# mLSTM attention and softplus feed-forward in one kernel: new places for the parts of the feature-major steps

## The chip, the cores and the metric

The kernel runs on one core of a Trainium2 chip, in one launch. The metric is device time in microseconds (us). TensorE (PE), VectorE (DVE), ScalarE (ACT) and GpSimd (POOL) compute; SyncE (SP) and ScalarE issue the DMAs.

## The reference

A gated linear recurrence (4 batches, 8 heads, 768 positions, head size 40) gives 3072 tokens of 320 features. Two matrix products with a softplus between them (320 to 2048 to 320) follow.

```python
for t in range(S):
    m_new = np.maximum(f_gate[:, :, t] + m, i_gate[:, :, t])
    f_stab = np.exp(f_gate[:, :, t] + m - m_new)
    i_stab = np.exp(i_gate[:, :, t] - m_new)
    C = f_stab * C + i_stab * einsum('bhd,bhe->bhde', vt, kt)   # state, 40x40 for each head
    n = f_stab * n + i_stab * kt
    y[:, :, t] = sigmoid(o_gate) * (C @ qt) / maximum(abs(n . qt), 1)
x = y as (3072, 320)
h = x @ w_in
out = (maximum(h, 0) + log1p(exp(-abs(h)))) @ w_out
```

## The kernel before

The recurrence is worked in chunks of 128 positions. One **step** is one chunk of one batch, with its eight heads; there are 24. Three steps make a **tile** of 384 tokens, and there are 8 tiles (`t` 0 to 7). While PE works through the feed-forward of one tile, it works the steps of later tiles in between.

**Feed-forward.** `products()` goes over 8 tiles and 16 **units** `f` of 128 hidden features each. A unit is eight matmuls into `hp` (line 929, from the high and low parts of the weights `wih`, `wil` and of the input `X`), then on ACT softplus twice (`gh`, rounded, line 806; `ab`, full, line 808), on POOL the low part `gl = ab - gh` (line 811), and nine matmuls into `po` (line 900): three with `gh` and `woh`, three with `gh` and `wol`, three with `gl`. The nine of a unit stand behind the eight `hp` matmuls of the unit two further on. `hp` has three buffers.

**Steps.** Tiles 0 and 1 use other forms of the step. From tile 2 on (`WIDE`) a step is feature-major (`wide_step`). For each tile `prepare` fetches q and k (`loq`, `lok`), rounds them on ACT (`hiq`, `hik`, line 277) and leaves the low parts in `loq`, `lok` by four subtractions on POOL (line 283). A step then has these parts:

- `load`: six copies of high and low parts to `qst`, `kst` (lines 364 and 365), the values `vt` (388), where needed a parked state `pk`.
- `decays`: two fetches `fb` (404); `decay`: two scans on DVE from them (`pw`, 413); `last_decays`: `gw` (434); `state_values`: `vw` on POOL (440).
- `scores` twice: four matmuls `sp` and a product on DVE (486). `stack`: the state's high part on ACT and low part on POOL (`cs`, 300 and 301). `state`: the matmuls `cp` (461). `old_state`, `new_state`: `cn` (452, 466) and its two copies by DMA (472, 473).
- `load_decays`: fetch into `y` (324, 325). `inter_wide` twice: matmuls `iq` and a product on DVE (540). `values_wide`: matmuls `yq`, a sum on DVE (553), then the result is written to DRAM (`yd`, 560, issued by ACT).
- `read_wide`: it is read back as `yx` and `nw` (564 to 568, issued by ACT). `finish_wide`: on DVE the normalizer `nm` and its product with the sigmoid of the output gate (`eg`, 572 to 576). `end_wide`: product on DVE (582), `X`'s high part on ACT (584), its low part on DVE (586).

**What sets the order.** A counter `n` counts the `hp` and `po` matmuls: 17 for a unit, 272 (`TS`) for a tile. A part is written into the program when `n` reaches the step's `base` plus the part's number (`W_SCAN`, `W_CP` and so on; a yield of -1000-r means r later than the last). Within each engine and each DMA queue the instructions run in the order in which they were written (`in_order`); across engines only data and buffers tie them. The bases of a tile's three steps stand 90 or 91 apart; in tile `t` the unit 0 begins at 272 t - 18. DMAs of SP and of ACT share eight completion semaphores in rotation, so that a DMA waits for the one eight before it.

**Sigmoids of the output gate.** `wide_gates` fetches `eg` for several tiles (three DMAs a tile), then loads another function table on ACT (335), takes the sigmoid (337) and loads the softplus table again (338). Before, it runs twice, for three tiles each, at `n` 150 and 1088.

Of the kernel before, what the change touches and what calls it, by code (L numbers as in the profile page):

```python
# [39 lines left out]
def mlstm_moe_kernel(  # L40
# [286 lines left out]
    def wide_gates(ts):  # L327

        yield 0
        for t in ts:  # L330
# [4 lines left out]
        nc.scalar.preload_act_table_set("sigmoid_and_others")
        for t in ts:
            nc.scalar.activation(eg[t], eg[t], AF.Sigmoid)
        nc.scalar.preload_act_table_set("softplus")
# [4 lines left out]
    eg = {}

    def load(z):
# [13 lines left out]
        else:  # L359
# [3 lines left out]
            for r, (a, e) in enumerate(((qh, kh), (qh, kl), (ql, kh))):  # L363
                nc.sync.dma_start(z.qst[r * D : (r + 1) * D].bitcast(F32), a[gs].bitcast(F32))
                nc.sync.dma_start(z.kst[r * D : (r + 1) * D].bitcast(F32), e[gs].bitcast(F32))
        if t > 0:
            z.old = None
            if z.c > 0 and not stays(z.b, z.c - 1):
                z.old = p2.tile([D3, H, E2], F32, tag="cn", name=f"pk{n}")
                for r in range(3 if t >= PLAIN else 1):  # L370
                    nc.sync.dma_start(z.old[r * D : (r + 1) * D], park[z.b])
# [170 lines left out]
    def values_wide(z):  # L542

        yq = ps_a.tile([PP + EP, HG, L], F32, tag="pa", name=f"yq{z.n}")
        for h in range(H):
# [13 lines left out]
        for i in range(2):
            nc.scalar.dma_start(rows[i], z.y[i * PP : i * PP + EP])  # L560
# [240 lines left out]
    def activation(t, f, hp, put):
        n = f"{t}_{f}"
        u = t * NF + f
        yield OF[0]
# [6 lines left out]
        (nc.vector if u >= NT * NF - GV else nc.gpsimd).tensor_tensor(gl, ab, gh, op=ALU.subtract)  # L811
# [212 lines left out]
```

## Time and profile before

| | |
|---|---|
| median of three runs | 552.43 us (550.63 to 556.28) |
| span of the profiled execution | 553.0 us; the page has no other time for it |
| busy in the span | PE 488.4 us (88%), DVE 304.7 (55%), POOL 256.0 (46%), ACT 197.3 (36%) |
| tile 0 of the feed-forward begins | 37.0 us |
| tiles 1 to 7 begin | 137.4, 199.0, 260.7, 323.9, 384.4, 448.8, 502.8 us |
| last `po` matmul ends | 549.6 us |

A row of the timeline gives the start in us, the duration, engine, line, operation, tiles and shapes, and in brackets how long the engine was idle before it and what ended that. The rows of stretches give for each engine the time busy, then the granted share of the PE clock. PE is busy most of the time, and its idle time is spread over places in every tile.

### The profile page before, as it was taken

Reading aid. Unit: us, or ns where it says so; the run is one execution under the profiler, and the core shown is the slowest. Engines: PE = TensorE matmul, PEld = TensorE weight load, DVE = VectorE, ACT = ScalarE, POOL = GpSimd, SP = SyncE. Lnnn points to the kernel's source line nnn. Section 1 sums busy time; section 2 is a strip of 40 time slices with the busy share of each in tenths; the row PEclk is TensorE's granted clock in tenths of the full one; section 3 lists DMA queues with packets and bytes.
Section 4 is the critical chain, followed back from the end, with each engine's and each line's share of the span. In section 5 each row is a group of like instructions: output and inputs, shape, how many; then the busy total and the mean of one; then the engine's idle time right before and its main releaser. Section 6 shows DMA issues by size and latency. Waiting matters only on the chain.

```text
span 553.0 us, 9162 instructions
## 1 busy us (share of the span) xinstructions
PE 488.4 (88%) x3368; PEld 461.4 (83%) x3368; DVE 304.7 (55%) x473; ACT 197.3 (36%) x401; POOL 256.0 (46%) x284
## 2 busy tenths in 40 slices
PE   7478878798996979899889979898998979999997
PEld 7457768697995979898878979798987979999997
DVE  7778887978627464475254564376254563551001
ACT  2426425364333223433223327433223323333332
POOL 4233344734628553475328653484427643533320
PEclk9859959859999889999898999899799989999999
...
GB/s 199 212 145 188 198 227 176 274 109 144 141 187 199 174 44 137 205 183 144 89 194 145 191 197 168 197 183 141 74 189 150 201 80 133 106 35 37 0 1 37
DMA packets 66143, 80.64 MB, mean 146 GB/s; under 512 B 8034, under 2 KB 47122, under 8 KB 66098
## 3 DMA queue, kind: packets, MB, share of 16 engines
...
q14 instruction: 18, 0.15, 0.1%
...
## 4 chain that ended last, share of the span: by engine, by line
PE 47%; DMA 16%; DVE 15%; issue 8%; POOL 7%; ACT 4%; SPq 3%; POOLq 0%; DVEq 0%; ACTq 0%
PE hp L929 19%; PE po L900 19%; DVE pw L413 3%; DMA cn<-cn 3%; PE yq L548 3%; DMA qst<-loq 2%; PE sp L484 2%; PE cp L461 2%; POOL loq L283 2%; POOL cs L301 2%; DMA loq<-in_qk 1%; DMA eg<-in_oT 1%; DVE y L553 1%; DMA yd<-y 1%; PE iq L537 1%
## 5 line engine op out<-in xcount | busy, mean ns | idle before, releaser
L811 POOL TENSOR_TENSOR gl<-ab,gh 128x384 fp32r<-128x384 f32 x123 | 137.5, 1121 | 171.3 <-ACT ab L808 164.8
L929 PE MATMUL hp<-X,wih 128*128 128x384 f32 x768 | 192.4, 354 | 19.1 <-DVE X L586 14.7
L929 PEld LDWEIGHTS hp<-X,wih 128*128 128x128 f32 x768 | 138.3, 197 | 25.0 <-DVE X L586 16.5
L806 ACT ACTIVATE gh<-hp 128x384 fp32r<-128x384 f32 x128 | 63.0, 493 | 250.8 <-PE hp L929 200.7
L900 PE MATMUL po<-woh,gh 128*128 128x320 f32 x384 | 86.6, 324 | 1.7 <-ACT woh L249 1.1
L900 PE MATMUL po<-woh,gl 128*128 128x320 f32 x384 | 84.9, 320 | 2.1 <-POOL gl L811 2.1
L900 PE MATMUL po<-wol,gh 128*128 128x320 f32 x384 | 84.9, 321 | 1.2 <-DVE wol L252 1.2
L413 DVE TENSOR_TENSOR_SCAN pw<-fb,ident 128x512 f32<-128x512 f32 x48 | 65.4, 1398 | 31.8 <-DMA fb<-fz_d 30.4
L900 PEld LDWEIGHTS po<-woh,gh 128*128 128x128 f32 x384 | 67.9, 197 | 3.8 <-ACT woh L249 1.7
L929 PE MATMUL hp<-X,wil 128*128 128x384 f32 x256 | 70.3, 355 | 0.0
L900 PEld LDWEIGHTS po<-wol,gh 128*128 128x128 f32 x384 | 64.6, 196 | 2.9 <-DVE wol L252 1.4
L900 PEld LDWEIGHTS po<-woh,gl 128*128 128x128 f32 x384 | 63.8, 193 | 3.4 <-POOL gl L811 3.1
L808 ACT ACTIVATE ab<-hp 128x384 f32<-128x384 f32 x128 | 62.4, 487 | 0.8 <-POOL vi L422 0.8
L540 DVE TENSOR_TENSOR y<-iq,y 41x512 f32<-41x512 f32 x36 | 24.6, 683 | 65.7 <-PE iq L537 64.1
L929 PEld LDWEIGHTS hp<-X,wil 128*128 128x128 f32 x256 | 47.7, 197 | 1.0 <-issue 0.9
L486 DVE TENSOR_TENSOR pw<-sp,pw 128x512 f32<-128x512 f32 x48 | 31.7, 682 | 19.8 <-PE sp L484 19.7
L484 PEld LDWEIGHTS sp<-qst,kst 120*128 120x128 f32 (+2 forms) x240 | 36.3, 213 | 3.8 <-issue 2.4
L484 PE MATMUL sp<-qst,kst 120*128 120x128 f32 (+2 forms) x240 | 37.1, 292 | 2.0 <-DMA kst<-in_qk 2.0
L440 POOL TENSOR_TENSOR vw<-vt,gw 128x328 f32<-128x328 f32 x19 | 18.6, 980 | 37.7 <-DVE gw L434 30.0
L301 POOL TENSOR_TENSOR cs<-cn,cs 120x336 fp32r<-120x336 f32 x15 | 19.7, 1311 | 24.3 <-ACT cs L300 20.1
L461 PEld LDWEIGHTS cp<-vw,vt 128*40 128x40 f32 x304 | 14.5, 127 | 18.8 <-POOL vw L440 12.5
L461 PE MATMUL cp<-vw,vt 128*40 128x41 f32 x304 | 16.7, 214 | 14.0 <-POOL vw L440 10.5
...
## 6 DMA issues: line engine op xcount, KB each, us to landing
fb<-fz_d SPq DMA_DIRECT2D x44, 256.0 KB
...
```

What stands on the lines that cost most here:

```text
L301: nc.gpsimd.tensor_tensor(z.cs, z.old, z.cs, op=ALU.subtract)
L413: nc.vector.tensor_tensor_scan(pw.rearrange(flat), fb.rearrange(flat), ident4.rearrange(flat), 0.0, ALU.mult, ALU.add)
L440: nc.gpsimd.tensor_tensor(z.vw, v1, z.gw.broadcast_to([128, H, E]), op=ALU.mult)
L461: nc.tensor.matmul(z.cp[:, h, :], z.kt[:, h * D : (h + 1) * D], z.vw[:, h, :], start=True, stop=True)
L484: nc.tensor.matmul(sp[:, j, :], z.kst[:, h, :], z.qst[:, h, :], start=True, stop=True)
L486: nc.vector.tensor_tensor(z.pws[i], sp, z.pws[i], op=ALU.mult)
L540: nc.vector.tensor_tensor(y, iq, y, op=ALU.mult)
L806: nc.scalar.activation(gh, hp, AF.Softplus)
L808: nc.scalar.activation(ab, hp, AF.Softplus)
L811: (nc.vector if u >= NT * NF - GV else nc.gpsimd).tensor_tensor(gl, ab, gh, op=ALU.subtract)
L900: nc.tensor.matmul(po[j], a[:, j * 128 : (j + 1) * 128], w[:, f, :], start=(f == 0 and left[j] == 2), stop=(last and left[j] == 0),)
L929: nc.tensor.matmul(hp, a, r, start=(i == 0), stop=(i == len(seq) - 1))
```

## The change

The numbers of the parts of a feature-major step are new, and so are some of the places. Line numbers behind are in brackets.

- **Fetches first.** `fb`, `vt` and a parked state are fetched 72 ahead of the base (before 22 and 48), `qst` and `kst` at 60, or 56 or 44 for a tile's first step (before 48 and 45), `y` at 12 ahead (before 17 behind). The scan stays at 4. The first feature-major step of all has its own places.
- **The state's stack** `cs` is at 10 instead of -6. `sp`'s second half, `cp`, `iq`, `yq` lie further apart.
- **The end of a step** comes earlier: `read_wide` starts at 114 instead of 107, but `finish_wide` is at 143 and `end_wide` at 154, where they were at 163 and 183 (137 and 157 for tile 2). The DMAs that ACT issues for write and read are spread by 5 or 6 instead of back to back, the small read `nw` first.
- **prepare**: the fetch is 131 ahead of the first step's base (121 for tile 3) instead of 106; the rounding follows 42 later instead of 24, the four subtractions 7 apart instead of 14. All four now stand ahead of the copy of k's low part into `kst`. Before, that copy stood ahead of k's subtractions for each tile's first step, so its rows held k itself.
- **Sigmoids** are taken for one tile at a time, in tiles 0 to 5: six runs of `wide_gates` instead of two. `eg` has two buffers instead of three.
- The engine of `gl` is written without the name `GV`; the condition is the same.

```diff
-    (W_LOAD, W_FB, W_SCAN, W_CN, W_CS, W_VW, W_SP0, W_SP1, W_Y, W_CP, W_CD,
-     W_IQ0, W_IQ1, W_VI, W_YQ, W_YD, W_RD, W_NM, W_FIN) = (
-        -48, -22, 4, 19, -6, 4, 6, 14, 17, 31, 47, 50, 62, 38, 68, 79, 107, 119, 139,
+    (W_FB, W_LOAD, W_Y, W_SCAN, W_VW, W_SP0, W_CS, W_SP1, W_CN, W_CP, W_VI, W_CD,
+     W_IQ0, W_IQ1, W_YQ, W_YD, W_RD, W_NM, W_FIN) = (
+        -72, -60, -12, 4, 4, 6, 10, 18, 22, 33, 40, 45, 46, 59, 76, 84, 114, 143, 154,
     )
-    PRD, PSY = 24, 14
+    PRD, PSY = 42, 7
-    GP = [150, 1088]
+    GP = [150, 95]
...
         for i in range(2):
             nc.scalar.dma_start(rows[i], z.y[i * PP : i * PP + EP])
+            yield 6
     def read_wide(z):
+        z.nq = p1.tile([128, L], F32, tag="sig", name=f"nw{z.n}")
+        nc.scalar.dma_start(z.nq, z.yd[DM : DM + H].partition_broadcast(128 // H))
         z.yx = stage.tile([128, 3, L], F32, tag="sg", bufs=3, name=f"yx{z.n}")
+        yield 5
         nc.scalar.dma_start(z.yx[:, 0:2], z.yd[0:256].rearrange("(c p) t -> p c t", p=128))
         for i in range(2):
+            yield 5
             nc.scalar.dma_start(z.yx[i * 64 : (i + 1) * 64, 2], z.yd[256:DM])
-        z.nq = p1.tile([128, L], F32, tag="sig", name=f"nw{z.n}")
-        nc.scalar.dma_start(z.nq, z.yd[DM : DM + H].partition_broadcast(128 // H))
...
     def wide_step(z):
-        yield W_LOAD if z.g else -45
+        first = z.s == WIDE * NG
+        if not first:
+            yield W_FB
+            decays(z)
+            load_values(z)
+            load_state(z)
+        yield W_LOAD if z.g else W_LOAD + (16 if z.t == WIDE + 1 else 4)
         load(z)
-        yield W_FB
-        decays(z)
+        if first:
+            yield -27
+            decays(z)
+            load_values(z)
+            load_state(z)
+        yield W_Y
+        load_decays(z)
         yield W_SCAN
         decay(z)
...
-        d = AWAY if z.t > WIDE else NEAR
-        ev += [(W_NM + d, lambda: finish_wide(z)), (W_FIN + d, lambda: end_wide(z))]
+        ev += [(W_NM, lambda: finish_wide(z)), (W_FIN, lambda: end_wide(z))]
-    AWAY, NEAR = 44, 18
...
-        (nc.vector if u >= NT * NF - GV else nc.gpsimd).tensor_tensor(gl, ab, gh, op=ALU.subtract)
+        (nc.vector if t * NF + f >= NT * NF - 5 else nc.gpsimd).tensor_tensor(gl, ab, gh, op=ALU.subtract)
...
-                    start(prepare(z.t), base - 106)
+                    start(prepare(z.t), base - (121 if z.t == WIDE + 1 else 131))
-        start(wide_gates(range(WIDE, WIDE + 3)), GP[0])
-        start(wide_gates(range(WIDE + 3, NT)), GP[1])
+        for t in range(WIDE, NT):
+            start(wide_gates([t]), TS * (t - 2) + GP[t > WIDE])
```

**Place 1: DVE where tile 4 of the feed-forward begins.** `X4` is its input, `eg4` the gate of its last step (batch 2, chunk 2, written `2_2`, is the next tile's first step, and `2_3` its second). Before:

```order
L553 TENSOR_TENSOR y2_2_3263<-yq2_2_3376,y2_2_3263 112x512
L572 TENSOR_SCALAR nm2_1_3394<-nw2_1_3257 128x128
L573 TENSOR_TENSOR nm2_1_3394<-nw2_1_3257,nm2_1_3394 128x128
L574 RECIPROCAL nm2_1_3394<-nm2_1_3394 128x128
L576 TENSOR_TENSOR eg4_980<-eg4_980,nm2_1_3394 128x384
L582 TENSOR_TENSOR eg4_980<-yx2_1_3253,eg4_980 128x384
L413 SCALAR_TENSOR_TENSOR pw2_3_0_3433<-fb2_3_0_3386,ident4_79 128x512
L413 SCALAR_TENSOR_TENSOR pw2_3_1_3435<-fb2_3_1_3388,ident4_79 128x512
L434 TENSOR_TENSOR gw2_3_3440<-gT_93,pw2_3_0_3433 128x4
L434 TENSOR_TENSOR gw2_3_3440<-gT_93,pw2_3_1_3435 128x4
L586 TENSOR_TENSOR X4_2969<-eg4_980,X4_2969 128x3x128
```

Now, at the same place:

```order
L579 TENSOR_SCALAR nm2_1_3362<-nw2_1_3282 128x128
L580 TENSOR_TENSOR nm2_1_3362<-nw2_1_3282,nm2_1_3362 128x128
L581 RECIPROCAL nm2_1_3362<-nm2_1_3362 128x128
L583 TENSOR_TENSOR eg4_2357<-eg4_2357,nm2_1_3362 128x384
L544 TENSOR_TENSOR y2_2_3196<-iq1_2_2_3377,y2_2_3196 41x512
L589 TENSOR_TENSOR eg4_2357<-yx2_1_3284,eg4_2357 128x384
L593 TENSOR_TENSOR X4_2921<-eg4_2357,X4_2921 128x3x128
L557 TENSOR_TENSOR y2_2_3196<-yq2_2_3410,y2_2_3196 112x512
L417 SCALAR_TENSOR_TENSOR pw2_3_0_3452<-fb2_3_0_3270,ident4_79 128x512
L417 SCALAR_TENSOR_TENSOR pw2_3_1_3454<-fb2_3_1_3272,ident4_79 128x512
```

The low part of `X4` has moved from behind the two scans to ahead of them and of the sum for `y`.

**Place 2: ACT in the middle of tile 3**, where `prepare` rounds q and k of tile 5 (`hiq5`, `hik5`). Before:

```order
L806 ACTIVATE gh3_5_2972<-hp3_5_2961 128x384
L808 ACTIVATE ab3_5_2974<-hp3_5_2961 128x384
L300 ACTIVATE cs2_1_2981<-pk2_1_2851,lowk_84 120x336
L584 CAST X4_2969<-eg4_980 128x3x128
L277 CAST hiq5_3001<-loq5_2938 120x1024
L277 CAST hik5_3017<-lok5_2940 120x1024
L564 DMA yx1_5_3022<-yd1_5_2950 128x2x128
L566 DMA yx1_5_3022<-yd1_5_2950 64x128 x2
L568 DMA nw1_5_3026<-yd1_5_2950 128x1x128
L806 ACTIVATE gh3_6_3039<-hp3_6_3009 128x384
```

Now:

```order
L277 CAST hiq5_2980<-loq5_2886 120x1024
L820 ACTIVATE gh3_5_2983<-hp3_5_2971 128x384
L822 ACTIVATE ab3_5_2985<-hp3_5_2971 128x384
L277 CAST hik5_3005<-lok5_2888 120x1024
L300 ACTIVATE cs2_1_3012<-pk2_1_2803,lowk_84 120x336
L820 ACTIVATE gh3_6_3040<-hp3_6_3019 128x384
...
L569 DMA nw1_5_3056<-yd1_5_2966 128x1x128
...
L820 ACTIVATE gh3_7_3096<-hp3_7_3068 128x384
...
L335 ACT_TABLE_LOAD
L337 ACTIVATE eg5_3051<-eg5_3051 128x1152
L338 ACT_TABLE_LOAD
L820 ACTIVATE gh3_8_3141<-hp3_8_3122 128x384
```

The two roundings are no longer side by side, the reads stand between later units, and a sigmoid with its two tables stands between units 7 and 8.

**Place 3: POOL in the middle of tile 3**, the same units. Before:

```order
L301 TENSOR_TENSOR cs2_1_2981<-pk2_1_2851,cs2_1_2981 120x336
L440 TENSOR_TENSOR vw2_1_2987<-vt2_1_2855,gw2_1_2984 128x328
L811 TENSOR_TENSOR gl3_5_3006<-ab3_5_2974,gh3_5_2972 128x384
...
L452 TENSOR_TENSOR cn2_1_3034<-pk2_1_2851,flast_91 40x8x41
L283 TENSOR_TENSOR loq5_2938<-loq5_2938,hiq5_3001 120x512
L811 TENSOR_TENSOR gl3_6_3051<-ab3_6_3041,gh3_6_3039 128x384
L283 TENSOR_TENSOR loq5_2938<-loq5_2938,hiq5_3001 120x512
...
L811 TENSOR_TENSOR gl3_7_3089<-ab3_7_3076,gh3_7_3074 128x384
L283 TENSOR_TENSOR lok5_2940<-lok5_2940,hik5_3017 120x512 x2
L811 TENSOR_TENSOR gl3_8_3139<-ab3_8_3122,gh3_8_3120 128x384
```

Now:

```order
L444 TENSOR_TENSOR vw2_1_2995<-vt2_1_2801,gw2_1_2992 128x328
L301 TENSOR_TENSOR cs2_1_3012<-pk2_1_2803,cs2_1_3012 120x336
L825 TENSOR_TENSOR gl3_5_3015<-ab3_5_2985,gh3_5_2983 128x384
L283 TENSOR_TENSOR loq5_2886<-loq5_2886,hiq5_2980 120x512 x2
...
L456 TENSOR_TENSOR cn2_1_3048<-pk2_1_2803,flast_91 40x8x41
L283 TENSOR_TENSOR lok5_2888<-lok5_2888,hik5_3005 120x512
L825 TENSOR_TENSOR gl3_6_3064<-ab3_6_3042,gh3_6_3040 128x384
L283 TENSOR_TENSOR lok5_2888<-lok5_2888,hik5_3005 120x512
...
L825 TENSOR_TENSOR gl3_7_3113<-ab3_7_3098,gh3_7_3096 128x384
```

`vw` has moved ahead of `cs`, and three of the four subtractions stand between `gl` of unit 5 and `gl` of unit 6, where one stood.

More of the change, by code (lines that the diff above doesn't have):

```diff
@@ L148, in later_gates @@
         yield GR[0]
-        m = p1.tile([NCHAIN, w + 1], F32, tag="eg", bufs=3, name="m")
+        m = p1.tile([NCHAIN, w + 1], F32, tag="eg", bufs=2, name="m")
         nc.vector.tensor_copy(m[:, 0:1], m_end)
@@ L330, in wide_gates @@
         for t in ts:
-            eg[t] = p1.tile([128, NG, 3, L], F32, tag="eg", bufs=3, name=f"eg{t}")
+            eg[t] = p1.tile([128, NG, 3, L], F32, tag="eg", bufs=2, name=f"eg{t}")
             for g in range(NG):
@@ L365, in load, with load_state @@
                 nc.sync.dma_start(z.kst[r * D : (r + 1) * D].bitcast(F32), e[gs].bitcast(F32))
+            return
         if t > 0:
[L367 to L371, printed above, removed]
+            load_state(z)
         if z.s != NG:
             load_values(z)
+    def load_state(z):
+        z.old = None
+        if z.c > 0 and not stays(z.b, z.c - 1):
+            z.old = p2.tile([D3, H, E2], F32, tag="cn", name=f"pk{z.n}")
+            for r in range(3 if z.t >= PLAIN else 1):
+                nc.sync.dma_start(z.old[r * D : (r + 1) * D], park[z.b])
     def load_values(z):
@@ L760, in wide_step @@
     def wide_step(z):
-        yield W_LOAD if z.g else -45
-        load(z)
-        yield W_FB
-        decays(z)
+        first = z.s == WIDE * NG
[5 more added lines that the diff above has]
+        yield W_LOAD if z.g else W_LOAD + (16 if z.t == WIDE + 1 else 4)
+        load(z)
+        if first:
+            yield -27
+            decays(z)
+            load_values(z)
+            load_state(z)
+        yield W_Y
+        load_decays(z)
         yield W_SCAN
@@ L776, in wide_step @@
         c = new_state(z)
-        ev = [(W_Y, lambda: load_decays(z))]
+        ev = []
         if not last:
@@ L786, in wide_step @@
             ev += [(W_IQ0, lambda: inter_wide(z, 0)), (W_IQ1, lambda: inter_wide(z, 1))]
-        ev += [(W_VI, lambda: gate_values(z)), (W_YQ, y), (W_YD, lambda: next(yw, None)), (W_RD, lambda: read_wide(z))]
-        d = AWAY if z.t > WIDE else NEAR
-        ev += [(W_NM + d, lambda: finish_wide(z)), (W_FIN + d, lambda: end_wide(z))]
+        ev += [(W_VI, lambda: gate_values(z)), (W_YQ, y), (W_YD, lambda: yw), (W_RD, lambda: read_wide(z))]
+        ev += [(W_NM, lambda: finish_wide(z)), (W_FIN, lambda: end_wide(z))]
         ev.sort(key=lambda e: e[0])
```

2 lines of the change are left out of this document (removed).

## The prediction

> **What bounds the kernel now.** I read the stretches first, one for each tile of the feed-forward from tile 1 on, then the waits, then the chain and the timelines at the two places in a tile where PE stands still. A row of the stretches has its length, then PE's busy time; the last three columns are the granted clock, the DMA share and GB/s.
>
> ```profile
> span 553.0 us, 9162 instructions
> 137.40:199.00 61.60, 57.20 (x422) 53.87 (x420) 34.03 (x51) 20.40 (x44) 32.85 (x36) 0.97 0.61 168
> 199.00:260.70 61.70, 56.57 (x419) 53.52 (x418) 32.36 (x50) 19.67 (x43) 33.63 (x39) 0.97 0.55 153
> 260.70:323.90 63.20, 56.78 (x403) 54.29 (x402) 31.57 (x47) 19.42 (x43) 31.00 (x36) 0.95 0.58 158
> 323.90:384.40 60.50, 55.08 (x401) 52.77 (x401) 33.05 (x47) 25.18 (x48) 33.33 (x36) 0.97 0.66 178
> 384.40:448.80 64.40, 57.94 (x418) 54.68 (x418) 32.42 (x50) 19.62 (x43) 32.81 (x39) 0.95 0.53 147
> 448.80:502.80 54.00, 51.07 (x350) 49.33 (x349) 25.70 (x36) 16.68 (x39) 23.78 (x26) 0.97 0.25 72
> 515.89 1.31 PE po L900 x9
> 517.20 1.39 PE hp L929 x8
> ```
>
> PE bounds tiles 1 to 7. In tile 7, with no step beside it, a unit takes 1.31 + 1.39 = 2.70 us; 16 of them are 43.2 us. The rest of a tile's 60 to 64 us is the steps' own matmuls and idle time. Length less busy time, PE is idle 4.40, 5.13, 6.42, 5.42, 6.46 and 2.93 us in tiles 1 to 6, 30.8 us in all. No other engine is near its limit: the next, DVE and POOL, have at most 34 us of work in a tile.
>
> ```profile
> PE hp L929 <- DVE X L586: 14.7, 6, 2.9
> DVE pw L413 <- DMA fb<-fz_d: 30.4, 12, 7.5
> ACT hiq L277 <- DMA loq<-in_qk: 23.2, 5, 6.7
> POOL vw L440 <- DVE gw L434: 30.0, 14, 5.1
> POOL cs L301 <- ACT cs L300: 22.2, 9, 6.9
> PE cp L461 <- POOL vw L440: 10.5, 7, 3.3
> ```
>
> Of the 30.8 us, 14.7 are one wait, repeated where a tile begins: `hp` for the low part of `X`. I call the other 16.1 us the middle. Its largest wait is `cp` for `vw`, and the rows above it show the chain behind: `vw` waits for `gw`, that for the scans, the scans for their fetch.
>
> **Where a tile begins.** The chain at the start of tile 2, then the slow restart at tile 6, then PE at tile 4.
>
> ```profile
> 197.86 0.56 DVE eg L582
> 198.42 3.01 DVE pw L413 x2
> 201.42 0.78 DVE gw L434 x2
> 202.21 0.48 DVE X L586
> 202.73 1.68 PE hp L929 x5
> 204.41 1.60 PE po L900 x6
> 452.50 1.97 PE hp L929 x5
> 327.48 0.62 PE L929 MATMUL hp<-X,wih 128*128 128x384 f32 x2 [2.78 <-DVE X L586]
> 327.93 0.51 PE L929 MATMUL hp<-X,wil 128*128 128x384 f32 x2
> 328.27 0.33 PE L929 MATMUL hp<-X,wih 128*128 128x384 f32 x1
> ```
>
> The scans and `gw`, 3.8 us, stand between the product (198.42) and the low part (202.21): the wait is an order on DVE, not missing data. Behind it PE runs slowly. Five `hp` matmuls took 1.68 us where a clean unit takes 5/8 of 1.39, or 0.87, and six `po` 1.60 where 6/9 of 1.31 is 0.87: 1.5 us lost at tile 2. At tile 6 the five took 1.97; I take 1.6 us for each of tiles 3, 5 and 6. Tile 4 loses 0.1 (its five end by 328.44, after 0.96). Gaps and restarts: **14.7 + 1.5 + 3 x 1.6 + 0.1 = 21.1 us.**
>
> The Trainium skill, in TensorE: Matmul & The Clock Gate, section Why this matters for your kernels, would have PE fall to half its clock only for idle gaps over about 3 us. By that rule the restarts would cost nothing, the term would be 14.7 and the sum 6.4 us smaller. The low part's wait, at most 2.9 us, did slow PE at tile 2, and one of 2.78 did not; the rows decide.
>
> **The change, part by part.**
>
> *The end of a step at 154 instead of 183.* On DVE the low part of `X` now stands ahead of the scans, in tiles 3 to 7 about 28 numbers before the tile begins (base 272 t - 200, so 272 t - 46 against 272 t - 18). At 2.70 / 17 = 0.16 us and more for each number that is over 4.4 us for a product, a cast and a subtraction, 0.56 + 0.5 + 0.48 us with nothing large between. The 3.8 us of scans fall behind the tile's start; what they feed, `sp` and `cp`, comes later too. Tile 2 has no such lead: its end moves from 157 to 154 only. There the cast on ACT stands behind the writes of `yd`:
>
> ```profile
> 195.82 1.24 ACTq L560 DMA_DIRECT2D yd<-y  x2
> 197.94 0.49 ACT L808 ACTIVATE ab<-hp 128x384 f32<-128x384 f32 x1
> ```
>
> After `ab` (198.4) come the two issues (1.24), the cast (0.5) and the low part (0.5): 200.7, against 199.8, where PE wanted it. I keep 0.9 us. **This part: -21.1 + 0.9 = -20.2.** It costs nothing more as long as `nw` and `yx` have landed by 143 and 154. From the first read to the normalizer there were 56 numbers and are now 29, or 5 us.
>
> *Fetches first, cs later, casts.* The middle, as the trace of tile 2 has it, and the gap of tile 3:
>
> ```profile
> 221.51 0.38 SPq L272 DMA_DIRECT2D loq<-in_qk  x1
> 224.52 1.23 DVE L413 TENSOR_TENSOR_SCAN pw<-fb,ident 128x512 f32<-128x512 f32 x1 [2.61 <-DMA fb<-fz_d]
> 228.53 1.05 ACT L277 CAST hiq<-loq 120x1024 fp32r<-120x1024 f32 x1 [3.42 <-DMA loq<-in_qk]
> 291.30 0.87 PE L461 MATMUL cp<-vw,vt 128*40 128x41 f32 x16 [3.35 <-POOL vw L440]
> L283 POOL TENSOR_TENSOR loq<-loq,hiq 120x512 fp32r<-120x512 f32 x12 | 15.7, 1304 | 5.3 <-ACT hiq L277 5.3
> L452 POOL TENSOR_TENSOR cn<-cn,flast 40x328 f32<-40x328 f32 x13 | 11.4, 880 | 0.0
> ```
>
> With `fb` fetched 76 numbers ahead of its scan (before 26), `vw` ahead of `cs`, and `cs` 50 numbers behind the copies of the state it is made from instead of 32, the waits that now end last there go. At stake are the 16.1 us of idle time and, as single gaps reach 3.35, I add three restarts of 1.6: **21 us**. What is late next is `gl`. POOL has three subtractions and `cn` between `gl` of units 5 and 6: 3 x 1.30 + 0.88 = 4.8 us, with `gl` itself (about 1) 5.8, while PE uses one unit, 2.7 us and the steps' matmuls, say 3.2. It depends on how late ACT is. `loq` took 228.53 - 221.51 = 7.0 us from issue to cast. The cast now stands 42 numbers behind its fetch instead of 24: 8.2 us at an estimated 53 us a tile (43.2 and the steps' matmuls). SP was behind its place by 3 us: number 57 of tile 2 falls at 199.0 + 75 x 0.2 + 4.4 (gap and restart) = 218.4. It has much the same copies ahead of the fetch now. So the cast waits 7.0 + 3.1 - 8.2 = 1.9 us instead of 4.6 (23.2 in five). PE's slack against a late `gh` is at least 3.8 us (next fence), and all `po` matmuls together waited 2.1 us for `gl`. The burst takes 5.8 of 3.2 + 3.8 = 7.0 us, which leaves 1.2 for a wait of 1.9: 0.7 short. Bounds for a tile: nothing, or, if the cast waits as it did, 3.4 us and a restart of 1.6. I take 1.6, nearer the lower, in each of five tiles. **-21 + 8 = -13.**
>
> *Sigmoids per tile.* Tile 4 shows a whole run of the old kind on ACT:
>
> ```profile
> 336.32 1.28 ACT L335 ACT_TABLE_LOAD   x1
> 337.62 3.27 ACT L337 ACTIVATE eg<-eg 128x1152 f32<-128x1152 f32 x3
> 340.91 1.28 ACT L338 ACT_TABLE_LOAD   x1
> 342.20 0.49 ACT L806 ACTIVATE gh<-hp 128x384 fp32r<-128x384 f32 x1
> 338.05 0.34 PE L929 MATMUL hp<-X,wih 128*128 128x384 f32 x1
> L900 PE MATMUL po<-woh,gl 128*128 128x320 f32 x384 | 84.9, 320 | 2.1 <-POOL gl L811 2.1
> 117.06 0.90 DVE L252 TENSOR_TENSOR wol<-sgo,woh 128x320 fp32r<-128x320 f32 x2 [3.23 <-ACT woh L249]
> ```
>
> `gh` began at 342.20 for an `hp` that had ended at 338.39: 3.8 us late, and PE did not stand still for it. A run for one tile is 1.28 + 1.09 + 1.28 = 3.7 us, shorter than the 5.8 that was hidden. In tile 0 the run of three delayed the weights (DVE idle 3.23 us), and it shortens by 2.2: **-2.2**, bounds 0 and -5 (six fetches fewer there too). In tiles 1 to 5 it now falls into the middle; I charge 0.5 us in four, **+2**, bounds 0 and 3.7 each.
>
> The Trainium skill (ScalarE: Activation LUTs, Rules for kernel authors) says the opposite of this edit: group functions by table set and finish one before the next; its What ACT_TABLE_LOAD costs gives 2.66 us for each switch, 1.28 of load and 1.38 of drain. Eight more loads would be 21 us of ACT by it. The rows have 1.28 us and the sigmoid 0.02 us behind the load, so 10 us, no drain.
>
> *The rest.* `gl`'s engine is unchanged: nothing. The ACT issues spread by 5 or 6 numbers cost the same sequencer time in smaller pieces: nothing, covered by the same slack. k's low part ahead of its copy: SP now waits for POOL where POOL waited for SP, some 60 numbers ahead of its use: nothing, covered by that distance (0.16 us and more a number).
>
> **Sum.** -20.2 - 13 - 2.2 + 2 = -33.4. From 553.0: 519.6. The median of the runs is 0.6 below this execution, so **519 us**.
>
> **Rivals.**
>
> *The middle goes altogether* (SP earlier than I think, no wait at the casts): 553 - 20.2 - 21 - 2.2 = 509.6. For it: both the fetch and the scan's causes are gone. Against it: the clump on POOL.
>
> *The middle stays, with `gl` in `cp`'s place*, because `loq` still lands late and the subtractions are clumped: 553 - 20.2 - 2.2 + 2 = 532.6. For it: 23.2 us of waiting at the casts, and the fetch still stands behind nine others.
>
> *The beginning does not do what it says.* The reads land behind the normalizer's new number, DVE waits there, and the low part is late again: the 21.1 stay, 553 - 13 - 2.2 + 2 = 539.8. Against it: `nw` was waited for on DVE three times only.
>
> *Slower.* ACT carries the cast's wait (4.6) and, two units on, the sigmoid (3.7): 8.3 us against a slack of 3.8, so `gh` is 4.5 late, POOL's burst adds 3.4, and two restarts 3.2: 11.1 for each of five tiles, against 21 / 5 = 4.2 that the middle costs now. 553 + 5 x 6.9 - 22.4 = 565. It decides from a middle of 4.2 + 22.4 / 5 = 8.7 us a tile. By the Trainium skill's 2.66 a switch (the page above) it would come at once, 2.7 us more a run.
>
> **How the numbers follow.** The forecast 0.48 (510 to 531, between its neighbours), middle gone 0.15, middle stays 0.18, beginning not cured 0.08, both of these at once, no change, 0.04, slower 0.07. The range 505 to 541 leaves out the last two and the far edges. Less than 1% is about what a measurement of this kernel cannot tell from nothing. Faster by over 1%: 0.88; within 1%: 0.05; slower: 0.07.
>
> **What would show it.** Right: no idle time ahead of `hp` for `X` in tiles 3 to 7, about 1 us at tile 2; no wait of the scans for `fb`; tiles 1 to 5 of 55 to 58 us; table loads with no gap on PE behind them. Wrong: `po` waiting for `gl` several us in units 5 to 8 (the cast's wait unchanged), or DVE waiting for `nw`. Most of the sum is gaps removed from one engine; if the chain behind a gap is as long by another way, PE only waits elsewhere, and that would make it wrong.

## The result, and the profile after

The changed kernel takes 531.59 us (median of four, 530.24 to 533.6) against 552.95 before (550.63 to 556.28). The ratio is 0.960, 95% interval 0.9545 to 0.9657: faster by 4%, where I had forecast 519 us and 6%. Each ratio below is to executions of the kernel before on the same chip, so ratios are compared, not microseconds. They come from undisturbed executions alone; in the run with tile 3's sigmoids later these are two of four, the profiled one is not among them, and of its tile lengths only tile 1's is given.

The stretches after, one for each tile from 0 to 6, with the columns of before:

```profile
span 528.5 us, 9150 instructions
36.60:137.03 100.43, 83.64 (x526) 74.46 (x527) 82.49 (x139) 45.91 (x90) 40.45 (x41) 0.83 0.60 176
137.03:201.28 64.25, 57.72 (x418) 53.22 (x416) 31.21 (x50) 23.68 (x46) 29.58 (x36) 0.97 0.56 160
201.28:256.53 55.25, 54.66 (x416) 52.05 (x417) 32.38 (x50) 22.51 (x45) 31.21 (x38) 1.00 0.64 180
256.53:314.29 57.76, 54.34 (x403) 51.27 (x402) 34.76 (x47) 22.89 (x46) 31.37 (x35) 1.00 0.62 175
314.29:372.68 58.39, 55.34 (x403) 52.76 (x401) 33.55 (x49) 23.57 (x46) 32.43 (x36) 0.97 0.62 173
372.68:428.54 55.86, 54.46 (x419) 51.97 (x417) 34.92 (x50) 23.29 (x45) 32.53 (x39) 1.00 0.66 180
428.54:479.08 50.54, 49.86 (x355) 48.43 (x353) 24.23 (x36) 17.09 (x39) 21.83 (x26) 1.00 0.28 81
```

The span is 24.5 us shorter. Tile 0 is as long as it was (100.4), tile 1 is 2.6 us longer (61.6 before), and tiles 2 to 6 are 26.0 us shorter: 277.8 against 303.8. The rest, 1.2 us, lies ahead of tile 0 and in tile 7. In tiles 2 to 6 PE's idle time falls from 26.4 us to 9.1, and its busy time by another 8.8, because it is granted its full clock in four of the five.

The waits after:

```profile
DVE nm L579 <- DMA nw<-yd: 13.2, 8, 6.4
DVE eg L589 <- DMA yx<-yd: 12.1, 6, 4.0
PE po L914 <- ACT ob L963: 7.8, 5, 3.0
```

The wait of `hp` for the low part of `X` (14.7 us before) is gone but for 0.67 us at tile 2 (there for the high part), and so are the scans' wait for `fb` (30.4) and that of `cp` for `vw` (10.5). A wait stands on PE that was not there: `po` for `ob`, 7.8 us. `ob` is ACT's copy of the finished `po`, which frees its PSUM for the next tile. ACT at the beginning of tile 4:

```profile
322.20 0.37 ACTq L572 DMA_DIRECT2D yx<-yd  x1
322.62 0.43 ACT L963 COPY ob<-po 128x320 f32<-128x320 f32 x1 [2.25 <-DMA fb<-fz_d]
325.70 0.48 ACTq L575 DMA_DIRECT2D yx<-yd  x1
326.22 0.43 ACT L963 COPY ob<-po 128x320 f32<-128x320 f32 x1 [3.18 <-DMA qst<-hiq]
326.70 0.41 PE L914 MATMUL po<-woh,gh 128*128 128x320 f32 x1 [3.04 <-ACT ob L963]
```

The two copies now stand between the three issues of the read `yx`, each of which needs one of the eight semaphores that it shares with SP; what ends the idle time ahead of the second copy is the landing of a copy of `qst`. The second copy comes 3.6 us behind the first, and PE stands still 3.04 us for it. From the first `hp` of unit 2 to that of unit 3 it takes 6.19, 7.17, 4.67 and 3.95 us in tiles 3 to 6, and 3.00 in tile 2, which has no such wait: 10.0 us in all.

### The profile page after: what moved, and what is told of

It reads as the page before. It is cut to its first block, busy times and chain, and to the rows that moved or that the text cites. A ratio compares the mean times of both kernels' runs of the same rounds, so it can differ in the third digit from the quotient of the medians.

```text
span 528.5 us, 9150 instructions
## 1 busy us (share of the span) xinstructions
PE 479.0 (91%) x3368; PEld 451.4 (85%) x3368; DVE 303.1 (57%) x473; ACT 207.0 (39%) x409; POOL 246.2 (47%) x284
## 4 chain that ended last, share of the span: by engine, by line
PE 53%; DMA 17%; DVE 10%; issue 6%; POOL 6%; ACT 4%; SPq 3%; ACTq 1%; POOLq 0%; DVEq 0%
PE hp L943 22%; PE po L914 22%; DMA qst<-hiq 4%; PE yq L552 3%; POOL gl L825 3%; PE sp L488 3%; DMA cn<-cn 2%; DMA y<-fc_d 2%; DMA kst<-in_qk 1%; PE iq L541 1%; DMA wr<-in_w_in 1%; DMA og<-in_vko 1%; PE yp L521 1%; DMA qst<-in_qk 1%; DVE wih L243 1%
## 5 line engine op out<-in xcount | busy, mean ns | idle before, releaser
L825 POOL TENSOR_TENSOR gl<-ab,gh 128x384 fp32r<-128x384 f32 x123 | 140.1, 1141 | 158.2 <-ACT ab L822 148.6
L943 PE MATMUL hp<-X,wih 128*128 128x384 f32 x768 | 189.0, 349 | 5.0 <-DVE wih L243 3.6
L820 ACT ACTIVATE gh<-hp 128x384 fp32r<-128x384 f32 x128 | 62.8, 491 | 173.8 <-PE hp L943 130.4
L914 PE MATMUL po<-wol,gh 128*128 128x320 f32 x384 | 87.3, 319 | 1.6 <-DVE wol L252 1.6
L914 PE MATMUL po<-woh,gl 128*128 128x320 f32 x384 | 82.9, 317 | 2.7 <-POOL gl L825 2.3
L417 DVE TENSOR_TENSOR_SCAN pw<-fb,ident 128x512 f32<-128x512 f32 x48 | 63.1, 1356 | 2.1 <-PE fb L403 2.1
L544 DVE TENSOR_TENSOR y<-iq,y 41x512 f32<-41x512 f32 x36 | 24.6, 683 | 42.2 <-PE iq L541 39.7
L488 PEld LDWEIGHTS sp<-qst,kst 120*128 120x128 f32 (+2 forms) x240 | 34.2, 203 | 5.9 <-DVE eg L589 2.5
L444 POOL TENSOR_TENSOR vw<-vt,gw 128x328 f32<-128x328 f32 x19 | 15.3, 806 | 50.7 <-DVE gw L438 44.2
L470 DVE TENSOR_TENSOR cn<-cn,cp 40x328 f32<-40x328 f32 x16 | 7.8, 487 | 38.3 <-POOL cn L456 26.2
L591 ACT CAST X<-eg 128x384 fp32r<-128x384 f32 x18 | 9.2, 514 | 38.4 <-DVE eg L589 37.9
L825 DVE TENSOR_TENSOR gl<-ab,gh 128x384 fp32r<-128x384 f32 x5 | 2.8, 559 | 34.7 <-ACT ab L822 34.7
```

Source lines behind the costliest of these rows:

```text
L417: nc.vector.tensor_tensor_scan(pw.rearrange(flat), fb.rearrange(flat), ident4.rearrange(flat), 0.0, ALU.mult, ALU.add)
L444: nc.gpsimd.tensor_tensor(z.vw, v1, z.gw.broadcast_to([128, H, E]), op=ALU.mult)
L488: nc.tensor.matmul(sp[:, j, :], z.kst[:, h, :], z.qst[:, h, :], start=True, stop=True)
L544: nc.vector.tensor_tensor(y, iq, y, op=ALU.mult)
L591: nc.scalar.copy(X[:, 0:3, ts], z.e)
L820: nc.scalar.activation(gh, hp, AF.Softplus)
```

## Experiments

The tile lengths (us) of the profiled executions, with the median of the runs and the ratio to before (553.0 to 557.2 us on the chips used). Of the three kernels with the middle end, tiles 2, 4, 5 and 6 agree within 0.7 us, tile 3 within 2.1; tile 0 differs by up to 5 us between kernels in which it is nearly the same.

| kernel | median | tile 0 | tile 1 | tiles 2 to 6 | their sum | ratio [95%] |
|---|---|---|---|---|---|---|
| before | 552.95 | 100.4 | 61.6 | 61.7, 63.2, 60.5, 64.4, 54.0 | 303.8 | 1 |
| changed | 531.6 | 100.4 | 64.3 | 55.3, 57.8, 58.4, 55.9, 50.5 | 277.8 | 0.960 [0.9545, 0.9657] |
| changed, old end | 530.0 | 102.5 | 67.1 | 55.5, 54.7, 54.9, 55.9, 50.5 | 271.5 | 0.957 [0.950, 0.963] |
| before, new end | 536.4 | 102.0 | 64.0 | 58.2, 57.7, 57.8, 58.8, 49.7 | 282.4 | 0.966 [0.959, 0.974] |
| reads late | 543.1 | 101.2 | 68.8 | 58.7, 56.5, 59.5, 60.4, 49.6 | 284.7 | 0.978 [0.970, 0.986] |
| sigmoids in two runs | 537.5 | 105.0 | 61.5 | 56.5, 58.4, 63.5, 55.2, 51.2 | 284.8 | 0.969 [0.960, 0.978] |
| late fetch | 534.9 | 100.1 | 68.8 | 55.1, 57.9, 55.3, 58.9, 50.1 | 277.2 | 0.967 [0.9625, 0.971] |
| cs early | 535.9 | 105.3 | 64.8 | 56.1, 58.3, 57.0, 58.5, 50.1 | 279.9 | 0.9665 [0.960, 0.973] |
| old prepare | 525.5 | 104.0 | 65.5 | 54.4, 53.5, 57.3, 54.2, 49.6 | 269.0 | 0.948 [0.944, 0.953] |
| middle end | 529.7 | 100.8 | 65.2 | 55.3, 58.4, 54.4, 55.1, 50.5 | 273.8 | 0.957 [0.952, 0.962] |
| late prepare | 531.3 | 105.4 | 65.2 | 55.6, 55.5, 60.0, 54.2, 49.6 | 274.9 | 0.957 [0.951, 0.964] |
| late prepare, middle end | 527.7 | 103.3 | 65.3 | 54.6, 56.3, 54.2, 55.1, 50.5 | 270.7 | 0.951 [0.946, 0.956] |
| tile 3's sigmoids later | 524.1 | | 60.7 | | | 0.945 [0.936, 0.954] |
| these three together | 526.4 | 104.3 | 62.8 | 54.6, 57.4, 54.2, 55.5, 50.5 | 272.1 | 0.948 [0.943, 0.952] |

### The end of a step alone, from both sides

The changed kernel with the old end:

```diff
-        ev += [(W_NM, lambda: finish_wide(z)), (W_FIN, lambda: end_wide(z))]
+        d = (20, 29) if z.t > WIDE else (-6, 3)
+        ev += [(W_NM + d[0], lambda: finish_wide(z)), (W_FIN + d[1], lambda: end_wide(z))]
```

> The changed kernel, with only the end of a feature-major step back at its old numbers (finish_wide at 163 and end_wide at 183; 137 and 157 for tile 2). Theory A (the beginning of a tile is a term by itself, set by where the end stands on DVE): the wait of hp for the low part of X comes back in tiles 3 to 7, 2.8 to 2.9 us each, with the slow clock behind it, so 531.6 + 5 x (2.9 + 1.6) - the 0.7 at tile 2 = 551 to 554 us at most, 546 with one restart in three as before. Theory B (with the earlier fetches the scans are no longer what stands ahead of the low part, so the old place costs little): 531 to 535 us.

The kernel before with the new end:

```diff
-        ev += [(W_NM + d, lambda: finish_wide(z)), (W_FIN + d, lambda: end_wide(z))]
+        ev += [(143, lambda: finish_wide(z)), (154, lambda: end_wide(z))]
```

> The kernel before, with only the end of a step at its new numbers (finish_wide 143, end_wide 154), reads and fetches as before. Theory A (my term for the beginning): 20.2 us off, 532 us, with no idle time ahead of hp for X in tiles 3 to 7, and the middle's waits of cp for vw unchanged at about 10 us. Theory B (the gap at the beginning only goes together with the other edits; alone DVE waits there for nw or yx, read at 107 and now used 36 earlier): 540 to 552 us.

In the kernel before, the new end takes 21.4 us off tiles 2 to 6, where I had forecast 20.2. The largest wait of PE that is left there is that of the middle:

```profile
PE cp L461 <- POOL vw L440: 8.6, 6, 2.1
```

So the term and its size hold; tile 1 grew by 2.4 us, and the whole kernel gained 3.4%. But taken back out of the changed kernel, the end costs nothing (0.957 against 0.960): theory A fell. DVE there at the beginning of tile 3:

```profile
256.24 0.23 DVE L579 TENSOR_SCALAR nm<-nw 128x128 f32<-128x128 f32 x1
259.31 0.69 DVE L557 TENSOR_TENSOR y<-yq,y 112x512 f32<-112x512 f32 x1 [0.34 <-PE yq L552]
259.92 0.55 DVE L589 TENSOR_TENSOR eg<-yx,eg 128x384 f32<-128x384 f32 x1
260.38 2.33 DVE L417 TENSOR_TENSOR_SCAN pw<-fb,ident 128x512 f32<-128x512 f32 x2
262.63 1.30 DVE L593 TENSOR_TENSOR X<-eg,X 128x384 fp32r<-128x384 f32 x1
```

The scans stand ahead of the low part as they did before, yet `hp` waits 0.70 us instead of 2.78. The sum for `y` has moved (`yq` from 68 to 76), so the normalizer, at the same 163, is now ahead of it and done while PE still works on `yq`. From the start of that sum to the end of the low part it is 4.6 us. In the kernel before it was 7.4:

```profile
256.74 0.69 DVE L553 TENSOR_TENSOR y<-yq,y 112x512 f32<-112x512 f32 x1 [1.36 <-PE yq L548]
257.35 0.22 DVE L572 TENSOR_SCALAR nm<-nw 128x128 f32<-128x128 f32 x1
259.98 3.09 DVE L413 TENSOR_TENSOR_SCAN pw<-fb,ident 128x512 f32<-128x512 f32 x2
263.00 1.18 DVE L586 TENSOR_TENSOR X<-eg,X 128x384 fp32r<-128x384 f32 x1
```

The end's new numbers suffice against this gap, and so do the other edits without them, but for 0.7 to 0.9 us in tiles 3 to 6. Tiles 3 and 4 are even shorter with the old end (54.7 and 54.9), since `po` does not wait for `ob` there.

### What makes po wait for ob

The reads of a tile's first step behind the copies of `ob`:

```diff
+        d = 0 if z.g else 18
-        ... (W_RD, lambda: read_wide(z))]
+        ev += [(W_RD + d, lambda: read_wide(z))]
-        ev += [(W_NM, lambda: finish_wide(z)), (W_FIN, lambda: end_wide(z))]
+        ev += [(W_NM + d, lambda: finish_wide(z)), (W_FIN + d, lambda: end_wide(z))]
```

> The changed kernel, with the read back, the normalizer and the end of each tile's first step 18 numbers later (132, 161, 172), so that on ACT its four reads stand behind the two copies of the finished po (ob) and not between them. Theory A (the reads on ACT's queue, which wait for a free semaphore of the DMAs, hold up the copies that free po): the wait of po for ob, 7.8 us in four tiles, and some 2 us of slow clock behind it go: 521 to 523 us. Theory B (something else would hold PE there, or the reads collide with the next ACT work): 529 to 533 us, the wait of gh or gl in the place of ob's.

The wait for `ob` went, and the kernel became slower than the changed one, neither of which theory alone had said. Its waits:

```profile
POOL vw L444 <- DVE gw L438: 60.8, 15, 8.2
DVE eg L589 <- DMA yx<-yd: 25.2, 10, 6.0
PE cp L465 <- POOL vw L444: 9.4, 3, 3.9
```

DVE now stands twice as long for `yx` (25.2 us, 12.1 in the changed kernel), ahead of the next step's scans; `gw`, `vw` and `cp` come late behind it, and the middle's gap is back, with 3.9 us in tile 4.

The end between its old and new numbers:

```diff
+        d = (17, 18) if z.t > WIDE else (0, 0)
-        ev += [(W_NM, lambda: finish_wide(z)), (W_FIN, lambda: end_wide(z))]
+        ev += [(W_NM + d[0], lambda: finish_wide(z)), (W_FIN + d[1], lambda: end_wide(z))]
```

> The changed kernel, with the end of a step between its old and new numbers, from tile 3 on (finish_wide 160, end_wide 172): the normalizer stands ahead of y's sum on DVE, the product with yx and the low part of X between that sum and the next step's scans. Theory A (the wait of po for ob comes from DVE: at 143 and 154 the wait for yx stands ahead of y's sum, so yd is written late, is read late, and ACT stands in the reads when ob is due; one wait feeds the other): the ob wait goes, the gap at the beginning stays gone, tiles 3 to 6 take 54.0 to 55.5 us each but the last: 521 to 525 us, ratio 0.940 to 0.952. Theory B (the ob wait only comes from the place of the reads in ACT's order, which is unchanged here): 529 to 533 us, ratio 0.955 to 0.965.

```profile
DVE nm L579 <- DMA nw<-yd: 5.8, 3, 4.6
DVE eg L589 <- DMA yx<-yd: 4.6, 2, 4.2
```

With ACT's reads where they were, `po` waits for `ob` no more, in this run and in the two others with this end. DVE's waits for `nw` and `yx` fall from 25.3 us to 10.4. How the one is tied to the other: DVE in the changed kernel, as tile 4 begins (314.29),

```profile
312.68 0.56 DVE L589 TENSOR_TENSOR eg<-yx,eg 128x384 f32<-128x384 f32 x1 [2.61 <-DMA yx<-yd]
314.29 0.68 DVE L557 TENSOR_TENSOR y<-yq,y 112x512 f32<-112x512 f32 x1
315.01 1.25 ACTq L564 DMA_DIRECT2D yd<-y  x2
```

and with the middle end, as the same tile begins (316.72):

```profile
314.17 0.69 DVE L557 TENSOR_TENSOR y<-yq,y 112x512 f32<-112x512 f32 x1 [0.34 <-PE yq L552]
314.78 0.55 DVE L589 TENSOR_TENSOR eg<-yx,eg 128x384 f32<-128x384 f32 x1
315.46 0.59 ACTq L564 DMA_DIRECT2D yd<-y  x1
325.89 0.42 ACT L964 COPY ob<-po 128x320 f32<-128x320 f32 x1 [2.07 <-DMA fb<-fz_d]
```

At 154 the product with `yx` stands ahead of the next step's sum for `y` and waits 2.61 us; the sum starts as the tile begins, and the write of `yd` behind it 0.7 us later. With the middle end the write starts 1.26 us before the tile begins, and the second copy of `ob` 9.2 us into the tile instead of 11.9. That is theory A's mechanism, and tile 4 is shorter by 4.0 us. But tile 3 kept other gaps (`gl` 1.04, `iq` 0.65 us), and the time is only 0.3% better, less than the intervals tell: theory B's range.

A late `yd` alone does not make the wait. In the kernel before with the new end, DVE waits 25.6 us for `nw`, and in tile 4 (from 318.04) `yd` is written 0.4 us into the tile, nearly as late as in the changed kernel:

```profile
318.45 1.31 ACTq L560 DMA_DIRECT2D yd<-y  x2
325.96 0.76 ACT L947 COPY ob<-po 128x320 f32<-128x320 f32 x2
```

But there the reads stand back to back at 107, the two copies of `ob` run together behind them, 7.9 us into the tile, and PE never waits for `ob`. So the wait seems to take both, the end at its new numbers and the reads at theirs; the old reads were not put back into the changed kernel.

### What took the middle away

`fb` late, behind the copies of `qst` and `kst`:

```diff
         if not first:
-            yield W_FB
+            yield W_LOAD if z.g else W_LOAD + (16 if z.t == WIDE + 1 else 4)
+            load(z)
+            load_state(z)
+            load_values(z)
+            yield -22
             decays(z)
-            load_values(z)
-            load_state(z)
-        yield W_LOAD if z.g else W_LOAD + (16 if z.t == WIDE + 1 else 4)
-        load(z)
         if first:
+            yield W_LOAD + 4
+            load(z)
...
```

> The changed kernel, with fb fetched at 22 ahead of the base again, and vt and the parked state behind the six copies of qst and kst, as before (the six copies, cs, prepare and the end as changed). Theory A (the early fetch is what took away the middle): the scans wait for fb again, cp waits for vw 2 to 3.4 us in tiles 2 to 5, and three or more restarts come back: 8 to 13 us more than the changed kernel, ratio to before 0.975 to 0.985. Theory B (the place of cs, and POOL's order, did it): 0 to 3 us more.

`cs` at -6:

```diff
-        -72, -60, -12, 4, 4, 6, 10, 18, 22, ...
+        -72, -60, -12, 4, 4, 6, -6, 18, 22, ...
```

> The changed kernel, with only the state's stack cs back at 6 ahead of the base (now 10 behind). Theory A (cs ahead of vw on POOL, waiting for its copies of cn, held vw up): cp waits for vw again, 1 to 2 us in tiles 2 to 5, 4 to 10 us more, ratio 0.968 to 0.978. Theory B (vw only ever waited for the scans): no difference, ratio 0.955 to 0.965.

Neither brings the middle back: in both, `cp` waits for `vw` once in tiles 2 to 6, 0.5 and 0.6 us. With the late fetch the scans wait for `fb` again, 20.2 us in thirteen, but PE feels it only once, in tile 1, where `sp` stands 6.1 us behind the waits of two scans, 3.40 and 2.90 us:

```profile
DVE pw L417 <- DMA fb<-fz_d: 20.2, 13, 4.2
```

With `cs` early the price is one stall in tile 0, where ACT stands 10.8 us for the state's copies, which SP issues only at 120.8:

```profile
125.24 0.57 ACT L300 ACTIVATE cs<-cn,lowk 120x336 fp32r<-120x336 f32 x1 [10.82 <-DMA cn<-cn]
```

As with the beginning, the rest of the change suffices in tiles 2 to 6 without either; what each alone is worth lies in tiles 0 and 1. The kernel before with only the new end, which has neither, keeps the gaps, but it lacks the other edits too; both taken back out of the changed kernel were not tried.

### Sigmoids

Two runs of three tiles:

```diff
-            eg[t] = p1.tile([128, NG, 3, L], F32, tag="eg", bufs=2, name=f"eg{t}")
+            eg[t] = p1.tile([128, NG, 3, L], F32, tag="eg", bufs=3, name=f"eg{t}")
...
-    GP = [150, 95]
+    GP = [150, 1088]
-        for t in range(WIDE, NT):
-            start(wide_gates([t]), TS * (t - 2) + GP[t > WIDE])
+        start(wide_gates(range(WIDE, WIDE + 3)), GP[0])
+        start(wide_gates(range(WIDE + 3, NT)), GP[1])
```

> The changed kernel, with the sigmoids taken in two runs of three tiles as before (eg with three buffers, runs at 150 and 1088). Theory A (the run in tile 1, with its fetches ahead of the six copies of qst and kst, makes ACT 8 us late there and sp wait): tile 1 gets 4 to 6 us shorter, tile 0 up to 2 longer, 526 to 530 us. Theory B (my terms, -2.2 and +2, which cancel; tile 1 is long because two of its steps stand 65 numbers apart and not 90): 530 to 533 us, tile 1 still 63 us or more.

```profile
318.91:382.43 63.52, 57.71 (x403) 54.21 (x401) 35.26 (x48) 25.31 (x47) 32.33 (x36) 0.95 0.64 177
346.86 1.05 ACT L277 CAST hiq<-loq 120x1024 fp32r<-120x1024 f32 x1 [7.43 <-DMA yd<-y]
```

Tile 1 gets 2.7 us shorter, where theory A had 4 to 6, but tile 4, which has the second run, gets 5.1 longer, and tile 0 4.6, no more than it differs between other kernels: 1.0% slower than the changed kernel, though the intervals overlap. In the kernel before, the long run left no gap on PE; here the cast that follows it in tile 4 waits 7.4 us, and PE 2.57 us for `gl` behind that. What of this is the run and what its nine fetches on SP was not separated.

Only tile 3's run, the one that falls into tile 1, later:

```diff
-            start(wide_gates([t]), TS * (t - 2) + GP[t > WIDE])
+            start(wide_gates([t]), TS * (t - 2) + (160 if t == WIDE + 1 else GP[t > WIDE]))
```

> The changed kernel, with only the sigmoid run of tile 3 (the one in tile 1) 65 numbers later, its fetches behind the six copies and its table loads near unit 12 of tile 1. Theory A (in tile 1 that run and its fetches make gh 8.7 us late and sp wait 2.2): tile 1 gets 3 to 5 us shorter, 60 to 61.5 us against 64 to 65 in the runs with the run in its new place, ratio 0.950 to 0.957. Theory B (tile 1 is long because its steps stand closer): no change, ratio 0.955 to 0.965, or the wait moves to the end of tile 1.

```profile
140.39:201.07 60.68, 55.62 (x418) 51.89 (x417) 33.04 (x50) 23.79 (x46) 29.53 (x36) 1.00 0.60 168
```

Tile 1 takes 60.7 us; in the nine profiles with that run in its new place it took 64.3 to 68.8. In the changed kernel its ACT shows why:

```profile
170.25 1.28 ACT L335 ACT_TABLE_LOAD   x1 [2.90 <-DMA yd<-y]
173.00 1.17 ACT L337 ACTIVATE eg<-eg 128x1152 f32<-128x1152 f32 x1 [1.46 <-DMA eg<-in_oT]
175.48 0.49 ACT L820 ACTIVATE gh<-hp 128x384 fp32r<-128x384 f32 x1
180.43 0.90 PE L488 MATMUL sp<-qst,kst 120*128 120x128 f32 x4 [2.23 <-DMA y<-fc_d]
```

The read `nw` holds ACT 2.9 us, the fetch of `eg` another 1.5, and `gh` of unit 8 begins 8.7 us after its `hp`; 3.8 us were hidden in the kernel before. Theory A holds. But the run is not all of it: with the run later, `sp` still waits 1.9 us at the same place, now for the scan, and the kernel before with the new end, which has no such run, takes 64.0 us for tile 1, with a wait of 2.9 us for `sp` there.

### The place of prepare

As before (the first step's rows hold k itself again):

```diff
-    PRD, PSY = 42, 7
+    PRD, PSY = 24, 14
-                    start(prepare(z.t), base - (121 if z.t == WIDE + 1 else 131))
+                    start(prepare(z.t), base - 106)
```

> The changed kernel, with prepare as before: the fetch of q and k 106 ahead of the first base, the cast 24 later, the subtractions 14 apart (so that the first step's rows hold k itself again). Theory A (the cast's wait on ACT counts: my term of 1.6 us for each tile): the cast waits 4 to 6 us in five tiles, po waits for gh or gl: 4 to 10 us more, ratio 0.967 to 0.98. Theory B (PE's slack against a late gh covers the cast's wait, whatever its length): ratio 0.955 to 0.965.

Faster than the changed kernel by 1.2%, the opposite of theory A and beyond theory B. The casts wait 7.0 us in all (17.6 in the changed kernel); `po` waits for `ob` 2.25 us in tile 4 and hardly elsewhere.

The same cast, but k's low part ahead of its copy:

```diff
-    PRD, PSY = 42, 7
+    PRD, PSY = 24, 7
...
-        yield W_LOAD if z.g else W_LOAD + (16 if z.t == WIDE + 1 else 4)
+        yield W_LOAD if z.g else W_LOAD + (16 if z.t == WIDE + 1 else 12)
...
-                    start(prepare(z.t), base - (121 if z.t == WIDE + 1 else 131))
+                    start(prepare(z.t), base - 106)
```

> The changed kernel, with prepare's fetch at 106 and the cast 24 later as before, but the subtractions 7 apart, and the first step's six copies at 48 ahead of its base (44 for tile 3), so that k's low part still stands ahead of its copy. Theory A (what made the run with the whole old prepare faster is the cast, 7 numbers later and so without a wait on ACT for loq or for loq's buffers): as fast as that run, ratio 0.943 to 0.953, casts waiting under 6 us in all. Theory B (it was the spread of the subtractions on POOL, or that SP did not wait for k's low part): back to the changed kernel, ratio 0.955 to 0.965, with gl late.

The casts wait 8.3 us, and the ratio is back at 0.957, though its interval just touches that of the old prepare: the cast's place is probably not the whole of it. `ob` costs 1.5 us in tile 3 and 3.05 in tile 4 again. Whether the spread of the four subtractions or SP's free way past k's low part makes the difference is open; the two were not tried apart.

### Together

The last kernel with the middle end, and with tile 3's run later too:

> The kernel with prepare as in the last one, and the end at 160 and 172 from tile 3 on. Theory A (two separate causes that make ACT and DVE late, and both feed the wait of po for ob): no ob wait at all, tiles 2 to 6 near 54.4, 53.5, 54, 54.5 and 49.8 us, 266 us together against 269 with the old prepare alone: ratio 0.938 to 0.95. Theory B (one and the same lateness, cured by either): no faster than the last one.

> The changed kernel with the three edits together: prepare at 106 with the cast 24 later (subtractions 7 apart, first copies at 48 ahead), the end at 160 and 172 from tile 3 on, and tile 3's sigmoid run 65 numbers later. Theory A (tile 1's loss to the sigmoid run is apart from what stands in tiles 2 to 6): the 4.3 us that tile 1 gained alone add to the run with the first two, 0.9513 - 4.3 / 554 = 0.9435, range 0.938 to 0.949, tile 1 at 60 to 61.5 us and no wait of po for ob. Theory B (the later run pushes its cost into tile 2 or the end of tile 1): 0.949 to 0.956.

The first gave 0.951: no wait for `ob`, tiles 2 and 4 where theory A has them, 5 and 6 0.6 and 0.7 us longer, tile 3 2.8: just outside its range. It is 0.6% better than the last kernel, less than the intervals tell, so theory B is not excluded. The second gave 526.4 us (525.3 to 528.4) and 0.948, at the edge of theory A's range, but its tile 1 is not in theory A's 60 to 61.5 us: it became 2.5 us shorter, where the later run alone had given 3.6. It beats both kernels, the changed one by 1.3% (their intervals do not overlap), but it is no faster than the old prepare alone, which has 0.948 too.

## Why the sign was right and the size too large

The spans differ by 24.5 us where the sum said 33.4. (The median missed by 12.6: I had also put it 0.6 us below the span, and it is 3.1 above.) The time is within 1 us of a rival's, the middle stays (532.6), but that is chance: the waits that it keeps are gone.

**The beginning, -20.2: right in size, wrong as a cause of its own.** The new end, added alone, gives -21.4 in tiles 2 to 6. But I took the order of scans and low part for the only cause; the other edits shorten the same chain by 2.8 us. The 0.9 us kept for tile 2 measured 0.67.

**Fetches and casts, -13: tiles 2 to 6 did better, tile 1 worse.** In tiles 2 to 6 the middle's gaps fell from 11.6 to 1.2 us; I had charged 1.6 us a tile for a clump on POOL. `po` waited for `gl` 2.3 us in all, where I had feared several us in units 5 to 8. The casts' wait was still there, 17.6 us in all (28.6 before), but PE's slack covered it at `gl`. In tile 1 the gaps grew from 4.4 to about 5.4 us; much of that goes when tile 3's sigmoid run is moved.

**"It costs nothing more as long as nw and yx have landed by 143 and 154": the step that failed.** They had not. DVE waited 13.2 us for `nw` (7.8 before) and 12.1 for `yx` (none before). I had named the wait for `nw` as what would prove me wrong, and weighed it at 0.08, as a return of the old gap. What it cost was another gap, `po` for `ob`, 10.0 us with its slow clock by the rows; without that wait tiles 2 to 6 were 4.0 us shorter with the middle end and 6.3 with the old one, as other gaps stay or come. I had costed the spread of ACT's reads at nothing, "covered by the same slack", without looking which ACT instruction has no slack: the copies of `ob` at a tile's beginning. In the kernel before, with the reads unspread, the same new end led to no such wait.

**Sigmoids, -2.2 and +2: both off.** Tile 0 gained nothing: what it may have gained it lost at its end:

```profile
123.72 0.58 ACT L300 ACTIVATE cs<-cn,lowk 120x336 fp32r<-120x336 f32 x1 [3.91 <-DMA cn<-cn]
126.53 1.28 PE L465 MATMUL cp<-vw,vt 128*40 128x41 f32 x16 [3.06 <-issue]
130.01 1.30 PE L943 MATMUL hp<-X,wih 128*128 128x384 f32 x3 [2.21 <-DVE wih L243]
```

ACT stands 3.9 us for the state's copies, and PE twice behind it; that the one causes the other was not tested. Tile 1 paid about 3.6 us for a run that I had at 0.5. Against two runs in this kernel the change may still be worth about 5 us (the intervals overlap).

**Sum.** In tiles 2 to 6 the end gives -21.4 and the wait for `ob` +10.0; what is left for the other edits is -14.6, which no run shows by itself. Tile 1 adds 2.6, and the edges -1.2: **-24.6** for the measured -24.5. The split hangs on the order: taken first, the other edits give -32.3 (changed kernel with the old end), and the new end then adds 6.3. Of the signs I had named, tiles 2, 3 and 5 are in 55 to 58 us, tile 4 0.4 beyond, tile 1 far outside; behind the table loads PE has a gap in tile 1 alone (0.81 us, for `gh`).

## What to carry to other kernels

Where an engine waits in a queue for DMAs, ask which instruction behind them has no slack; a wait that no one feels for most of a tile is felt at the one place where a buffer must be freed. A gap that two edits each remove does not come back when one is undone, so test an edit from both sides, added alone and taken out alone. When an end is moved up against a round trip through memory, try half the way too: here it took away most of DVE's wait and kept the gain, though it gained nothing clear of noise by itself.

## What the runs showed of the chip

PE's slow clock does not follow the length of a gap alone; it matters where the gap falls. In each of the fourteen traces the granted clock is full or half, and it changes only at moments that lie a whole number of 3.41 us apart. Below are stretches between such moments: behind the length stands PE's busy time, and the granted clock is the third number from the end. The kernel before has a gap of 2.78 us where tile 3 begins and another where tile 4 begins:

```profile
261.13:264.54 3.41, 0.63 (x4) 0.32 (x4) 3.41 (x4) 0.00 (x0) 2.63 (x2) 1.00 0.00 0
264.54:267.95 3.41, 3.41 (x15) 3.41 (x13) 0.23 (x1) 0.87 (x2) 1.00 (x1) 0.50 0.15 42
322.57:325.98 3.41, 2.12 (x14) 1.72 (x12) 3.38 (x3) 1.75 (x4) 2.46 (x2) 1.00 0.89 263
325.98:329.39 3.41, 1.91 (x13) 1.92 (x13) 2.04 (x5) 0.75 (x2) 1.86 (x2) 1.00 0.21 57
329.39:332.81 3.42, 3.42 (x28) 3.23 (x27) 0.83 (x2) 1.14 (x4) 1.82 (x4) 1.00 0.93 245
```

The gap of tile 3 lies in one stretch, and the next one has half the clock. That of tile 4 is divided over two, with 1.3 and 1.5 us idle, and costs nothing. Old prepare, with the gap of 2.25 us ahead of `po` in tile 4:

```profile
322.60:326.01 3.41, 1.19 (x8) 0.93 (x6) 0.00 (x0) 0.42 (x1) 0.00 (x0) 1.00 0.65 188
326.01:329.43 3.42, 3.40 (x14) 3.32 (x15) 1.96 (x4) 0.87 (x2) 1.47 (x1) 0.50 0.64 199
```

From 140 us on, over all fourteen traces, each of the 28 stretches at full clock in which PE was idle for 1.88 us or more was followed by one at half the clock, and none of the 1493 with 1.5 us or less; of the 15 between, 8 were. A half-clock stretch then loses at most 1.7 us, an estimate from its length of 3.41; the prediction took 1.6 for a restart. The Trainium skill (TensorE: Matmul & The Clock Gate, Why this matters for your kernels) speaks of gaps over about 3 us. By that none of these three gaps would have been followed by a slow clock; two were.
